# A windowed-attention and MLP kernel on one NeuronCore: the order replanned with later landings of batch 0's cast loads

## The chip, the cores and the metric

The kernel runs on one core of one Trainium2 chip. The metric is the device time of one execution in microseconds, lower being better; the figure for the kernel before is the median of 13 executions. The profile is of one further execution of the same program. Its engines are TensorE (PE; PEld is its weight load), VectorE (DVE), ScalarE (ACT), GpSimd (POOL) and SyncE (SP).

## The reference

Attention over 4 batches, 8 heads, 768 positions and head size 64, where each query sees the last 128 keys and the first 4 ("sinks"), is followed by a two-layer MLP with a squared ReLU on the 3072 tokens of 512 features:

```python
scores = scale * q @ k^T
keep   = (key position < 4) | (0 <= query - key < 128)
a      = softmax(where(keep, scores, -1e9))
x      = (a @ v), heads side by side: 3072 x 512
h      = x @ w_in                      # 512 -> 2048
out    = (max(h, 0) ** 2) @ w_out      # 2048 -> 512
```

All inputs and the output are float32.

## The kernel before

**Tiling.** A batch has six tiles of 128 positions, taken as three tile pairs (`s` or `u` = 0, 1, 2). For each batch the stages are: bring q and k into a layout with the head size on the partitions (`stage`, by PE transposes for batches 0 and 1 and by DMA transposes on SP's queue for 2 and 3); scores, exponential and mask; values and normalisation; the "bridge", which transposes the attention output for the MLP; `layer1` with ReLU and square; and `layer2`. Most of layer 2 is done by `layer2_fast`, which forms a tile pair with seven block products in place of eight, from sums of the squares (`sg`) and of the weights (`wt`). Attention of batch b+1 is interleaved with the MLP of batch b.

**Who does what.** PE runs all matmuls and transposes. ACT has the exponentials and most ReLUs; DVE has the normalisations, most squares, sums and copies out of PSUM. A multiplication by the window mask can be on DVE (L776) or on POOL (a pair of affine selects, L355). `sink_keys` (two small copies into `kblk`, L679) gathers the keys of the four sinks, `sink_scores` (L703) multiplies by them, `sink_exp` (L711) is their exponential, and every value product of tile pairs 1 and 2 reads the result. PSUM is divided into four tiles of two banks, two named "att" and two named "den".

**Loads.** q and k of batch 0, tiles 0 to 3, come as float32 through SP's queue and are cast ("regrouped") on DVE, ACT or POOL. Tiles 4 and 5 of batch 0 and all of the other batches, as v, w_in and w_out, are cast to bfloat16 by DMAs that POOL issues. `load_cast` issues those of q and k for batches 0 (tiles 4 and 5) and 1 (L507). The POOL queue's order is fixed by the program: v tiles 0 and 1, a quarter of w_in, v 2 and 3, the other three quarters of w_in, k and q tiles 4 and 5, v 4 and 5, w_out, and then batch 1. The DMAs of a queue follow one another in that order; where POOL's compute instructions stand between them is the planner's choice.

**What sets the order.** Nothing in the program is placed by hand at the end. Every piece of work is an `Op` with a key, the engines that can do it with an assumed cost, the ops that it follows and the buffers that it takes and frees. `Plan.run` repeatedly takes, of all ops that are ready, the one with the lowest (planned start + lag, key), chooses the engine that would end it first, and emits its instructions. `Plan.place` first moves the keys and lags: by group with `PLACES` (a shift, a scale and a lag for all ops of, say, the scores of batch 1's tile pair 0), and then one by one with `NUDGES`. The assumed times are only for planning: `LATENCY` is the assumed handoff between engines, and a DMA is assumed to land at

```python
end = queue[e] + DMA_LATENCY + o.margin
```

(L238). So the constants change no instruction by themselves; they change the order on each engine and the engine that some ops get. One thing depends on planned gaps directly: `warm` (L317) emits PE transposes of the identity, which compute nothing that is used, in front of an op for which PE is planned to wait, as long as the planned time is below `WARM_UNTIL`.

The function that the diff touches:

Of the kernel before, what the change touches and what calls it, by code (L numbers as in the profile page):

```python
# [16 lines left out]
LATENCY = 0.122  # L17
# [5 lines left out]
    ('att', 0, 0): (-2.46, 0.47, -0.66), ('att', 0, 1): (-0.14, 1.62, -0.14), ('att', 0, 2): (-1.375, 1.42, -0.64),  # L23
    ('att', 1, 0): (0.765, 0.89, 0), ('att', 1, 1): (-0.28, 2.29, -0.72), ('att', 1, 2): (0.08, 1.3, -0.06),
    ('att', 2, 0): (-0.07, 1.27, 0), ('att', 2, 1): (1.14, 0.56, -0.28), ('att', 2, 2): (-1.285, 1.05, -0.48),
    ('att', 3, 0): (0.09, 1.14, 0.06), ('att', 3, 1): (0.4, 1.06, -0.08), ('att', 3, 2): (-0.465, 1.16, -0.56),
    ('ev', 0, 2): (-0.46, 0.74, 0.02), ('ev', 1, 0): (-0.01, 0.91, -2.78), ('ev', 1, 1): (-0.165, 1.04, 0),
    ('ev', 1, 2): (-0.025, 0.87, 0.02), ('ev', 2, 0): (0.11, 0.96, 0), ('ev', 2, 1): (-0.045, 0.93, 0.36),
    ('ev', 2, 2): (-1.3, 0.62, 1.04), ('ev', 3, 0): (0.22, 2.01, -1.96), ('ev', 3, 1): (0, 1, -0.42),
    ('ev', 3, 2): (0.04, 1.07, -0.02), ('l1', 0, 0): (-0.28, 2.16, -0.32), ('l1', 0, 1): (-0.035, 0.33, -0.46),  # L30
    ('l1', 0, 2): (1.69, 0.27, -0.42), ('l1', 1, 0): (0.825, 0.61, -0.02), ('l1', 1, 2): (-0.155, 0.96, 0.14),
    ('l1', 2, 0): (0.035, 0.76, -0), ('l1', 2, 2): (-2.375, 1.53, -0.32), ('l1', 3, 0): (0.025, 1.07, -0.42),
    ('l2', 0, 0): (0.32, 2.21, -0.22), ('l2', 0, 1): (0.44, 1.69, 0.06), ('l2', 0, 2): (-4.315, 2.49, -0.54),
    ('l2', 1, 0): (0, 1.01, 0), ('l2', 1, 1): (2.345, 1.97, 0.22), ('l2', 1, 2): (-0.41, 0.56, 0.12),
    ('l2', 2, 0): (-0.41, 0.41, -0.6), ('l2', 2, 1): (-0.47, 0.26, 0.66), ('l2', 2, 2): (0, 1.01, 0),
    ('l2', 3, 0): (-0.09, 1.06, 0), ('l2', 3, 2): (-0.12, 0.72, 2.76), ('prep', 0, 0): (4.54, 2.5, -1),
    ('prep', 0, 1): (-1.04, 0.71, -0.64), ('prep', 1, 0): (0.935, 2.5, -0.44), ('prep', 3, 0): (-0.495, 2.45, 0.1),
    ('sink', 0, 0): (-0.755, 0.62, -0.54), ('sink', 0, 1): (0.135, 0.98, -0.04),
    ('sink', 1, 0): (-0.375, 1.71, 0.04), ('sink', 1, 1): (0.365, 0.61, 0.08), ('sink', 2, 0): (-0.01, 2.21, 0.06),
    ('sink', 3, 0): (-0.045, 0.9, 0), ('sum', 0, 2): (0, 1, -0.2), ('sum', 1, 0): (0.345, 0.25, -2.82),  # L40
    ('sum', 1, 1): (-0.27, 0.85, 0.08), ('sum', 1, 2): (-0.61, 0.73, -0.3), ('sum', 2, 0): (-0.06, 0.53, 1.32),
    ('sum', 2, 1): (-0.185, 1.13, 0.06), ('sum', 2, 2): (1.225, 2.25, -1.82), ('sum', 3, 0): (-0.005, 0.78, -0.5),
    ('sum', 3, 1): (-0.08, 0.34, 0.58), ('sum', 3, 2): (-0.185, 1.76, 0.42), ('turn', 0, 0): (4.705, 1.71, -0.76),
    ('turn', 0, 1): (0.09, 1.27, -0.04), ('turn', 0, 2): (1.185, 0.93, -0.3), ('turn', 1, 0): (0, 1.04, 0),
    ('turn', 1, 1): (0.995, 1.58, 0.4), ('turn', 1, 2): (0.65, 0.38, 0.02), ('turn', 2, 0): (0.67, 0.92, 0.14),
    ('turn', 2, 1): (-0.005, 0.93, -1.56), ('turn', 2, 2): (0.105, 1.4, 0.26), ('turn', 3, 0): (-0.1, 1.13, 0.08),
    ('turn', 3, 1): (-0.045, 0.55, -0.08), ('turn', 3, 2): (0.095, 1.46, -0.1),
    ('val', 0, 0): (-3.365, 0.71, -0.66), ('val', 0, 1): (0.145, 1.37, 0), ('val', 0, 2): (-1.82, 0.34, -3),
    ('val', 1, 0): (-0.355, 1.14, 0.04), ('val', 1, 1): (1.24, 2.09, -0.76), ('val', 1, 2): (0.18, 1.66, -2.5),
    ('val', 2, 0): (4.08, 1.76, -1.82), ('val', 2, 1): (0.05, 1.41, 0), ('val', 3, 0): (-1.585, 0.72, -0.38),  # L50
    ('val', 3, 1): (0.115, 0.58, -0.88), ('val', 3, 2): (-0.1, 1.09, -0.02), ('wt', 0): (0.275, 0.55, 0.32),
}
NUDGES = {
    4: (-0.366, 1.44), 16: (0, -0.3), 17: (0.072, -1.02), 18: (-0.061, -1.08), 19: (0.005, -0.02),
    20: (0.18, -0.98), 21: (0.025, -1.52), 24: (0, -0.44), 25: (-0.338, -1.38), 26: (0.71, 1.9),
    27: (-0.006, -0.32), 28: (0.484, 0.84), 29: (0, -0.36), 30: (-0.027, 0.14), 31: (0.007, -0.26), 32: (0, -0.48),
    33: (-0.136, -2.88), 34: (-0.096, 0.58), 35: (-0.031, 0.88), 36: (-0.018, 0), 37: (0.103, 0.12),
    39: (0.084, 0.7), 41: (-0.017, 0.88), 42: (0, -0.36), 43: (-0.11, 0.72), 44: (0, -0.12), 45: (0.297, 0.68),
    46: (-0.172, -1.86), 47: (-0.011, 0), 48: (-0.112, -0.02), 49: (-0.039, 1.08), 50: (-0.207, 0.22),
    51: (-0.044, 1.66), 52: (-0.002, -0.14), 53: (-0.017, -1.04), 54: (0, -0.2), 56: (-0.203, 0.34),  # L60
    58: (0.029, -0.48), 59: (0.008, 0), 60: (0.204, -1.22), 61: (0.19, 0.54), 62: (-0.101, -1.14), 63: (-0.022, 0),
    64: (0.192, 0.18), 65: (-0.153, 0.14), 66: (0.306, 0), 67: (0, -0.12), 69: (0.192, -2.78), 70: (-0.072, 0),
    71: (-0.012, 0), 72: (0, 0.38), 73: (-0.071, -0.04), 74: (-0.001, 0.16), 75: (-0.154, 0.08), 76: (0.133, -0.02),
    77: (0.57, 1.32), 78: (0.012, 0.46), 81: (-0.043, 0.3), 82: (0.016, -2.06), 83: (0.261, -0.22), 84: (-0.009, 0),
    86: (0.047, -0.02), 87: (0.257, -0.48), 88: (-0.361, 0.4), 89: (-0.047, 0.42), 90: (0.15, 0.34),
    91: (-0.217, 0), 92: (0, -0.06), 93: (0.05, -0), 94: (-0.016, 0), 95: (0.007, 0.02), 98: (0.071, -1.36),
    99: (-0.204, 0.84), 100: (0.062, -0.24), 101: (0, 0.08), 102: (0.126, 0.34), 103: (-0.194, -0.22),
    104: (0.051, 0), 105: (-0.214, -0.16), 108: (0.126, 0), 109: (0.206, 0), 110: (0.582, 0.28), 111: (0.032, 0.44),
    113: (-0.082, 0.1), 114: (-0.531, 0.32), 115: (0.058, -0.02), 116: (-0.003, -0.42), 118: (0.141, -1.44),
    119: (-0.307, 0.3), 120: (0.009, 0.06), 121: (0.002, 0), 122: (-0.044, 0.36), 123: (-0.017, 0.24),  # L70
    125: (-0.069, 0.34), 126: (0.099, -0.44), 127: (0, 0.14), 128: (-0.238, -0.62), 129: (-0.154, -0.08),
    130: (-0.003, 0), 131: (-0.296, 0.4), 132: (-0.082, -0.32), 133: (0.024, -0.38), 134: (0.073, 0),
    135: (0.059, 0.06), 136: (0.065, 0), 137: (0.021, 0.44), 138: (-0.166, 0.68), 139: (0.012, 0.3),
    140: (0.032, -0.28), 141: (-0.189, 0), 143: (0.103, 0), 144: (0.071, -0.44), 145: (-0.059, 0),
    146: (-0.436, 0.38), 148: (0.164, -0), 150: (0.527, -1.46), 151: (-0.19, 0.24), 153: (0.033, 0), 155: (0, 0.04),
    156: (0.089, 0), 157: (0.185, -0.32), 158: (-0.173, 0.56), 159: (-0.171, 0.18), 160: (0.252, 0.52),
    161: (-0.034, 1), 162: (-0.113, 1.42), 163: (0.013, 0.48), 165: (-0.127, 0.32), 166: (0.044, 0.4),
    167: (-0.035, 0.68), 169: (0, -0.14), 170: (-0.137, 0), 171: (-0.007, 0.26), 172: (0, 0.16),
    174: (-0.066, -0.92), 175: (0.19, 0.58), 177: (0.091, 0), 178: (0.319, -0.4), 179: (-0.18, 1.08),
    180: (-0.069, 0.02), 181: (-0.338, 0.2), 182: (-0.006, -0.02), 185: (-0.471, 1.5), 186: (-0.092, 0),  # L80
    187: (0.214, -0.08), 188: (0.107, -0.42), 189: (0.232, 0), 190: (0.088, 0), 192: (0, -0.16), 193: (-0.003, 0),
    194: (-0.01, -0.06), 196: (0.202, -0.16), 197: (0.001, -0.26), 198: (-0.511, 0), 199: (0.009, -1.34),
    200: (0.532, 0.1), 201: (-0.061, -1.16), 202: (-0.007, 0), 204: (-0.154, 0.18), 205: (0.379, 0.36),
    206: (-0.08, 0.86), 208: (0.012, -1.06), 209: (-0.163, -1.22), 210: (-0.013, 0), 211: (0.032, 0.04),
    212: (-0.121, 0), 213: (0, -0.2), 214: (0, 1.06), 215: (0, -0.06), 216: (0.121, 0.78), 217: (-0.108, 0),
    218: (0.25, 0.48), 219: (-0.155, 0), 220: (0.299, -0.24), 221: (0, -0.16), 222: (0, -0.3), 223: (-0.2, 0),
    224: (-0.065, 0), 225: (0, -0.38), 226: (0.019, -0.14), 228: (0.152, -0.9), 229: (-0.183, -0.86),
    230: (-0.164, 0), 231: (-0.021, 0.6), 232: (0.141, 0.18), 233: (-0.345, 0.26), 236: (0.132, -2.36),
    237: (0.017, -0.1), 238: (0, 0.72), 239: (-0.152, 0.14), 240: (-0.106, 0.48), 241: (-0.058, 0.3),
# [165 lines left out]
def kernel(  # L255
# [239 lines left out]
    def load_cast(b, tiles):  # L495

        for ti in (1, 0):
            for t in tiles:
                takes = []
# [726 lines left out]
```

## Time and profile before

| | us |
|---|---|
| median of 13 executions (216.68 to 217.8) | 217.06 |
| profiled execution, its own time | 217.19 |
| its span, from the first to the last instruction | 215.5 |
| PE busy in the span | 206.8 |
| DVE busy | 146.0 |
| ACT busy | 117.6 |
| POOL busy | 88.7 |

The profiled execution took 0.13 us more than the median, and 1.7 us of its time lie outside the span. Rows of the profile give the engine, the line of the kernel that made the instruction (which can be that of a helper: L331 is any copy on DVE, L329 any on ACT), what it writes and reads, and the times. A PE's end is modelled, so its busy time is an upper bound of the work. Waits name what ended them.

### The profile page before, as it was taken

To read this page: it belongs to the slowest core of one execution; us is meant where nothing else is said; L and a number is where in the kernel's file an instruction comes from. 1 tells how busy PE (TensorE), PEld (TensorE's weight loads), DVE (VectorE), ACT (ScalarE), POOL (GpSimd) and SP (SyncE) were. 2 spreads that over 40 slices of the span, in tenths; PEclk is the share of its full clock that TensorE was granted. 3 is DMA by queue.
4 is the path that set the end of the run, shared out by engine and by line. 5 is a ranking of instruction groups with operands and counts; after the bars stand their busy time and mean duration, and the time that the engine had idled before them with its cause. 6 is when DMAs were issued, how large, how long until landed. Compare 5 with 4: busy or idle time off the path is not lost.

```text
span 215.5 us, 5189 instructions
## 1 busy us (share of the span) xinstructions
PE 206.8 (96%) x2184; PEld 160.1 (74%) x2184; DVE 146.0 (68%) x276; ACT 117.6 (55%) x147; POOL 88.7 (41%) x127
## 2 busy tenths in 40 slices
PE   7789999999999999999999999999999999999992
PEld 7548987688667688554889765884988855799892
DVE  6588546697965866966788858779984543466652
ACT  3588667548864267778651627668411036656210
POOL 7999273598988963089405002227000000000000
PEclk9999999999999999999999999999999999999999
DMA  5999999999999999999969976020152220000222
GB/s 161 275 184 206 170 204 212 157 132 191 159 131 160 188 154 197 150 123 104 146 45 158 160 173 148 6 46 0 27 76 97 97 101 0 0 5 0 97 100 97
DMA packets 93351, 26.06 MB, mean 121 GB/s; under 512 B 86800, under 2 KB 91280, under 8 KB 93328
## 3 DMA queue, kind: packets, MB, share of 16 engines
q0 software_dynamic: 69248, 12.59, 76.4%
q1 hardware_dynamic: 23896, 13.07, 29.2%
q8 instruction: 17, 0.28, 0.5%
q10 hardware_dynamic: 184, 0.07, 0.1%
q14 instruction: 6, 0.05, 0.1%
HBM read 27.30 MB, written 6.29 MB: 156 GB/s over the span
## 4 chain that ended last, share of the span: by engine, by line
PE 81%; DMA 7%; POOL 4%; DVE 3%; SPq 1%; ACT 1%; issue 1%; POOLq 0%
PE pm L890 35%; PE py L1042 28%; PE py L931 6%; PE po L812 6%; DMA qn<-in_q_dram 5%; PE ps L744 4%; DMA qr<-in_k_dram 3%; SPq L486 1%; POOL qn L507 1%; PE pt L637 1%; POOL w_in_sb L443 1%; DVE qkT L331 1%; PE ya L1042 1%; PE px L861 1%; DVE r L903 1%
## 5 line engine op out<-in xcount | busy, mean ns | idle before, releaser
L890 PE MATMUL pm<-xT,w_in_sb 128*128 128x256 bf16 (+1 forms) x576 | 88.3, 309 | 0.3 <-ACT r L901 0.2
L890 PEld LDWEIGHTS <-w_in_sb 128*128 128x128 bf16 x576 | 62.4, 114 | 20.7 <-issue 2.1
L901 ACT ACTIVATE r<-pm 128x1024 bf16<-128x1024 f32 x41 | 42.0, 1024 | 39.4 <-PE pm L890 37.9
L764 ACT ACTIVATE expm<-ps 128x1024 bf16<-128x1024 f32 (+1 forms) x48 | 43.4, 951 | 12.0 <-PE ps L744 11.8
L912 DVE TENSOR_TENSOR gT<-r 128x1024 bf16<-128x1024 bf16 x34 | 24.1, 711 | 20.9 <-ACT r L901 20.5
L355 POOL TENSOR_SCALAR_AFFINE_SELECT expm<-expm 128x512 bf16<-128x512 bf16 x26 | 18.1, 722 | 44.7 <-ACT expm L764 37.3
L1042 PEld LDWEIGHTS <-gT 128*128 128x128 bf16 x336 | 31.3, 98 | 3.7 <-issue 0.3
L1042 PEld LDWEIGHTS <-sg 128*128 128x128 bf16 x240 | 22.8, 98 | 3.9 <-issue 0.9
L1042 PE MATMUL py<-wt,sg 128*128 128x256 bf16 x160 | 20.8, 273 | 0.1
L1042 PE MATMUL py<-wt,gT 128*128 128x256 bf16 x160 | 20.7, 273 | 0.0
L1042 PE MATMUL py<-w_out_sb,gT 128*128 128x256 bf16 x144 | 18.7, 273 | 0.0
L829 DVE TENSOR_TENSOR xn_sb<-po,rc 128x512 bf16<-128x512 f32 (+1 forms) x28 | 17.2, 615 | 1.0
L812 PEld LDWEIGHTS <-expm 128*128 128x128 bf16 x352 | 16.3, 97 | 1.8 <-issue 0.5
L812 PE MATMUL po<-v,expm 128*128 128x65 bf16 x352 | 17.2, 193 | 0.0
L776 DVE TENSOR_TENSOR expm<-expm,tri 128x1024 bf16<-128x1024 bf16 x19 | 13.2, 710 | 4.6 <-ACT expm L764 4.6
L931 PE MATMUL py<-w_out_sb,gT 128*128 128x512 bf16 x64 | 15.8, 380 | 0.0
L744 PE MATMUL ps<-qkT 64*128 64x128 bf16 (+1 forms) x256 | 14.8, 238 | 0.2 <-DVE xn_sb L829 0.2
L910 ACT ACTIVATE gT<-r 128x1024 bf16<-128x1024 bf16 x14 | 14.7, 1058 | 0.3
L744 PEld LDWEIGHTS <-qkT 64*128 64x128 bf16 x256 | 8.0, 94 | 7.8 <-issue 5.4
L329 ACT ACTIVATE osb<-py 128x256 f32<-128x256 f32 (+1 forms) x13 | 5.6, 433 | 13.2 <-PE py L1042 7.7
L812 PE MATMUL po<-vs,es 128*128 128x65 bf16 x128 | 12.6, 193 | 0.0
L545 POOL DMA_DIRECT2D v<-in_v_dram x12 | 10.7, 908 | 4.0 <-PE po L812 4.0
(79 smaller groups left out, 243.5 us busy)
## 6 DMA issues: line engine op xcount, KB each, us to landing
out_dram<-osb SPq DMA_DIRECT2D x11, 512.0 KB, 3.8
v<-in_v_dram POOLq DMA_DIRECT2D x24, 128.0 KB, 6.1
qn<-in_k_dram POOLq DMA_DIRECT2D x20, 128.0 KB, 7.2
qn<-in_q_dram POOLq DMA_DIRECT2D x20, 128.0 KB, 6.3
w_in_sb<-in_moe_w_in_dram POOLq DMA_DIRECT2D x4, 512.0 KB, 8.7
w_out_sb<-in_moe_w_out_dram POOLq DMA_DIRECT2D x4, 512.0 KB, 10.7
qr<-in_k_dram SPq DMA_DIRECT2D x4, 256.0 KB, 5.5
qr<-in_q_dram SPq DMA_DIRECT2D x4, 256.0 KB, 5.3
```

What stands on the lines that cost most here:

```text
L355: nc.gpsimd.affine_select(out=e_tile, in_=e_tile, compare_op=ALU.is_ge, fill=fill, base=i - 1, pattern=[[0, n], [1 if i else -1, 128]], ch ...
L744: nc.tensor.matmul(ps[:, h2, o:o + w], lhsT=qkT_sb[r, m, 1, c, :], rhs=qkT_sb[r, m, 0, qb:qb + w // 128, :], start=(i == 0 and not biased) ...
L764: nc.scalar.activation(out=x[:, :, o:512], in_=bank_t["s", b, s, m][:, :, o:512], func=AF.Exp, scale=scale)
L776: nc.vector.tensor_mul(y, y, tri.rearrange("p (o a) c -> p o (a c)", o=1).to_broadcast([128, 4, 256]))
L812: touch(("po", b, s, m0), e, nc.tensor.matmul(pv[:, i, h2, :], lhsT=lhsT, rhs=rhs, start=(n_ == 0), stop=(n_ == len(mms) - 1)), j)
L829: touch(("po", b, s, m0), e, nc.vector.tensor_tensor(out=xn_sb[:, 2 * s:2 * s + 2, 128 * (m0 + j0):128 * (m0 + j0 + nj)].rearrange("p i (j ...
L890: nc.tensor.matmul(pm[:, i, :], lhsT=w_in_sb[:, fb // 4, kb, fb % 4:512:4], rhs=xT[:, c0 // 256:(c0 + cw) // 256, kb, :], start=(kb == 0), ...
L901: nc.scalar.activation(out=o, in_=h, func=AF.Relu)
L910: nc.scalar.activation(out=g, in_=r, func=AF.Square)
L912: nc.vector.tensor_mul(g, r, r)
L931: touch((b, u), e, nc.tensor.matmul(pm[:, i, :], lhsT=gT_sb[t // 4][:, fb, 128 * (t % 4):128 * (t % 4) + 128], rhs=w_out_sb[:, fb, :], sta ...
L1042: ins = nc.tensor.matmul(y_, lhsT=x[:, i, :], rhs=r_, start=(first or tail and n == 2) and i == 0, stop=i == HB - 1, skip_group_check=not ...
```

## The change

The diff has three parts. `LATENCY`, the assumed handoff, goes from 0.122 to 0.135 us. The loads of `load_cast` get a margin: they are assumed to land 1.2 us later for batch 0 and 0.3 us later for batch 1. And `PLACES` and `NUDGES` are new throughout: another set of shifts and lags, so that the order on every engine is another one.

```diff
-LATENCY = 0.122
+LATENCY = 0.135
...
 PLACES = {
-    ('att', 0, 0): (-2.46, 0.47, -0.66), ('att', 0, 1): (-0.14, 1.62, -0.14), ('att', 0, 2): (-1.375, 1.42, -0.64),
...
+    ('att', 0, 0): (3.3, 1.08, 0.18), ('att', 0, 1): (3.285, 0.47, 0.38), ('att', 0, 2): (-0.2, 1.41, -0.24),
...
 NUDGES = {
-    4: (-0.366, 1.44), 16: (0, -0.3), 17: (0.072, -1.02), 18: (-0.061, -1.08), 19: (0.005, -0.02),
...
+    4: (-0.022, 0.56), 16: (0, 0.14), 17: (-0.211, -0.38), 18: (0.48, -1.62), 19: (0, 0.4), 20: (0.364, -0.58),
...
-                dma_op("pool", ("qk", b, ti, t), run, 0.9, None, takes)
+                dma_op("pool", ("qk", b, ti, t), run, 0.9, None, takes).margin = 0.3 if b else 1.2
```

What this does to the order, read from the two programs' instructions:

- The set of PE operations is the same; there are 61 warm-up transposes in place of 56. DVE has 239 planned operations in place of 233, ACT 148 in place of 146, POOL 86 in place of 94.
- Start: k and q of head pair 1 are transposed ahead of those of pair 2. POOL no longer casts k of head pair 3 (DVE does). On POOL, the triangles and the first window mask stand ahead of w_in 2 and 3 (the quarters are numbered from 0); they stood behind w_in 2. `sink_scores` of batch 0 moves from ahead of three of the four scores of tile pair 1 to behind all four, and `sink_exp` to behind three exponentials on ACT. The transposes of tiles 4 and 5 move behind one more layer-1 group.
- Batch 0, layer 2: tile pair 1 comes first, then pair 0 with pair 2; before, it was pair 0, then pair 1 with pair 2. SP's first store is now that of tile pair 1, and the store of tile pair 0 stands third, ahead of eight DMA transposes for batch 2.
- Batch 1: attention goes through tile pairs 0, 1 and 2 in that order; before, it was 1, 2, 0. Six of its eight first-group transposes stand together.
- Batches 2 and 3: the layer-2 pairs and the attention pieces are interleaved in another order. The last seven products, their evacuations and the last store are the same.

## The prediction

> **What bounds the kernel now.** I read the page's busy rows and slices first, then TensorE's waits, then the busy time by stretch, then the timelines of the first 30 us.
>
> ```profile
> span 215.5 us, 5189 instructions
> PE 206.8 (96%) x2184; PEld 160.1 (74%) x2184; DVE 146.0 (68%) x276; ACT 117.6 (55%) x147; POOL 88.7 (41%) x127
> PE   7789999999999999999999999999999999999992
> PEclk9999999999999999999999999999999999999999
> ```
>
> TensorE is busy for 96% of the span, at the full granted clock, and the slices below 9 are the first three and the last. All four batches' matmuls stay, so a new order can only take away time in which TensorE stands still, or add some. How much there is:
>
> ```profile
> PE pt L322 <- POOL ident L379: 1.5, 1, 1.5
> PE pt L637 <- DVE qs L331: 1.4, 1, 1.4
> PE pk L703 <- DVE kblk L679: 0.6, 1, 0.6
> PE pt L637 <- DMA qn<-in_q_dram: 0.5, 1, 0.5
> PE px L861 <- DVE xn_sb L829: 0.3, 1, 0.3
> PE pm L890 <- ACT r L901: 0.2, 1, 0.2
> PE ps L744 <- DVE xn_sb L829: 0.2, 1, 0.2
> ```
>
> Columns: who waited for whom, us in total, times, longest. All but the 0.2 for `r` lie before 30 us, and the stretches agree:
>
> ```profile
> 4.25:17.45 13.20, 10.74 (x148) 7.00 (x146) 9.29 (x20) 9.34 (x14) 12.43 (x22) 1.00 1.46 229
> 17.45:30.00 12.55, 12.09 (x156) 11.87 (x153) 6.94 (x20) 8.37 (x11) 7.75 (x11) 1.00 1.72 188
> 30.00:50.00 20.00, 20.00 (x215) 14.83 (x213) 14.42 (x24) 11.98 (x14) 13.68 (x19) 1.00 1.76 171
> 50.00:90.00 40.00, 39.65 (x471) 30.22 (x471) 29.95 (x57) 25.90 (x33) 28.54 (x37) 1.00 2.08 168
> ```
>
> Each row is a stretch, its length, then busy us of PE, PEld, DVE, ACT, POOL. PE idles 2.46 us from 4.25 to the first MLP matmul at 17.45, 0.46 from there to 30, 0.35 in 50 to 90, and nothing in the later stretches up to 211.5. So at most about 3.3 us can be won, most of it before 17.5 us, while the later 180 us can only lose. Three places matter before 30 us:
>
> ```profile
> 12.48 2.06 DVE L679 COPY kblk<-qkT 64x16 bf16<-64x16 bf16 x2
> ...
> 12.76 0.58 POOL L355 TENSOR_SCALAR_AFFINE_SELECT tri<-tri 128x128 bf16<-128x128 bf16 x2
> 13.27 1.23 POOL L355 TENSOR_SCALAR_AFFINE_SELECT expm<-expm 128x512 bf16<-128x512 bf16 x2
> ...
> 11.18 3.10 ACT L764 ACTIVATE expm<-ps 128x1024 bf16<-128x1024 f32 x4
> ...
> 28.97 0.45 PE L637 MATMUL pt<-ident,qn 128*128 128x128 bf16 x5 [0.46 <-DMA qn<-in_q_dram]
> ```
>
> (Start, us, instruction, [idle before it].) The two tiny sink-key copies take 2.06 us, until 14.54, while the same pair of batch 1 takes 0.83 (timeline, 55.97). The four normalisations behind them, each 0.6 (RECIPROCAL 0.17, TENSOR_TENSOR 0.42), start only at 14.57; they end at 16.84, and the bridge, its copies and layer 1 follow. The last line is the cast load of q tile 5, landing 28.93, for which TensorE stood 0.46.
>
> **The change, part by part.** The margin and LATENCY add no instruction: they alter planned times, and with the new PLACES and NUDGES the order. In instructions: the PE work is the same but for 61 warm-up transposes in place of 56, all before layer-1 group 4 of batch 0; about twice as many go where a wait was planned, so I price them at nothing in a wait and 5 x 0.06 = 0.3 at most. POOL loses its one CAST (0.6) and, net, seven mask pairs (1.23 each, 0.69 on DVE); DVE gains 6 operations and ACT 2. Neither DVE (68%) nor ACT (55%) becomes the bound by that.
>
> *To the first layer-1 matmul.* The transposes now come in the order in which q and k land (m0, m1, m2, m3, where m2's k stood ahead of m1). That fills the 1.4 us wait, but the last q load, regrouped on ACT at 10.64 (0.63), still gates m3's transposes (11.3 against 11.43), and v tile 1 lands at 12.46, where the first value product starts in both. So the 1.4 is worth nothing by itself: the landing and the exponentials are late next. ACT's four exponentials follow the regroup as before (11.2 to 14.4; with one done early and the bridge copy at 14.75). What moves is POOL and DVE. POOL no longer regroups; the triangles follow w_in 1 and run at about 11.0 to 11.5, and the mask on expm waits for its exponential, now third in ACT's row: 12.9 to 14.2. DVE reaches the sink keys at 12.4; the second copy starts at about 12.85, takes 0.17 to 0.43, and the norms go at 13.1, 13.7, 14.4 (behind its value product) and 15.1 (behind the exponential ending 14.5). From there: second bridge half 15.75 to 16.0, scores to 16.35, sink scores to 16.7, xT copy 16.55, layer 1 at 16.7 against 17.45. The sink exponential moved behind three others on ACT: 18.05 to 18.45, and all four value products of tile pair 1 need it, so they start at 18.5 where layer 1 left off at 18.45. Four of them at 0.365, with two warm-ups: second layer-1 group at 20.05 against 20.69, which is **-0.64**.
>
> One rule speaks against this. The row: 2.06 us for a pair that elsewhere takes 0.83, ending with POOL's last select at 14.50. The Trainium skill, "SBUF — State Buffer", section "Who interferes with whom", says a VectorE copy in a two-port mode and a GpSimd operation take a shared port pair as a lock, and the one issued later waits for the whole of the other. The row agrees (1.2 us longer), though a mask product at 62.52 under a POOL select took 0.88 against 0.68, less than a full wait. By the row alone the lock is gone with the overlap: -0.64. By the rule it depends on who starts first, copy at 12.85 or select at 12.9; if the select wins, norms start at 14.25, layer 1 at 17.7, the sink exponential at 19.25, the values at 19.7 and the next group at 21.2: +0.5. I take the first, since the copy is ahead by a hair.
>
> *To 30 us.* One more 1.75 us layer-1 group stands ahead of the tile-4/5 transposes, which come at about 29.3 (20.05 and 0.45 of bridge, then five groups at 1.75), behind the landing at 28.93. The 0.46 goes: **-0.46**. If the lock holds, the work is later by itself and 0.5 - 0.46 leaves 0.
>
> POOL's queue, which this reordering passes: w_in 2 and 3 were issued at 12.01 and 15.38 and now stand behind that mask, at about 14.2 and 15. The queue was behind (w_in 1 landed 19.08, w_in 2 21.69), and the shortest issue to landing seen on it is 4.1 (56.59 to 60.65), of which 0.85 is its own service: an issue before 19.08 - 3.2 = 15.9 delays nothing. Cost 0. The deadlines are 22.3 and 25.8.
>
> *30 to 211.5.* Here the order of batch 0's layer 2, and of batch 1 to 3, is new. The small waits of before (0.07 at 57.6, 0.20 at 78.4, 0.08 at 85.6) belong to their old neighbours: -0.35. New ones, by the order: six transposes now stand together before batch 1's sink scores; DVE has a relu (1.2), three copies (0.4), two squares (0.6 to the next start) and the key copies (0.83), 4.5 us, and waits 0.9 for the transposes between, 5.4 in all, against 5.27 of PE work (1.75 + 6 x 0.225 + 2 x 0.865 + 0.44) from the end of that relu's matmuls: +0.15. Bridge of batch 1's tile pair 0 to its layer 1, with only scores and sinks between: +0.15. Batch 2's second value product takes an "att" buffer that the bridge of batch 1 frees one copy (0.42) later, with 0.37 of work between its end and the handoffs: +0.33. These three are not in the trace of before; I bound them by 0 and 1.5 together, and take 0.63, near the waits of its own kind (0.07 to 0.6). Sum **+0.28**.
>
> SP: the store of batch 0's tiles 0 and 1 moves from first to third, behind matmuls at about 71, and eight DMA transposes queue behind it; at 1.3 to 2.2 issue each and 6.3 to land the fourth is there at about 86, needed at 94. Free. Layer 2's w_out tiles are wanted 3 us after they land (32.48, 34.94, 37.39, 39.84). The last product, its evacuations and stores have one order in both: the 3.9 us tail stays.
>
> Sum: -0.64 - 0.46 + 0.28 = -0.82. Against the profiled execution's 217.19 (span 215.5) that is 216.37; the runs' median lies 0.13 lower, 217.06, so **216.25**.
>
> **The rivals.**
> A. The lock holds: sink keys still end with the mask. For it: 0.05 us between the two starts. Against: POOL is idle from the triangles. Time: 217.06 + 0.0 + 0.28, about 217.3.
> B. Slower, by one mechanism: the w_in loads. If w_in 2's later issue is passed on whole (14.2 - 12.0 = 2.2 us), it lands at 23.9 and not at 22.3 where it is wanted, everything behind it in the queue shifts too, and q tile 5 lands at 31.1 against 29.3: +1.8 for -1.1 won, 217.06 + 0.7 + 0.28, about 218.0. It decides from an issue later than 15.9. Against it: the backlog.
> C. The batch-1 block, 46 to 95 us, gives the gain back: the three new waits reach their bound of 1.5, and VectorE's queue slips once by a relu (1.2) in front of a copy that TensorE needs: 217.06 - 1.1 - 0.35 + 2.7, about 218.3. For it: PE has only four tiles of PSUM to run ahead in. Against: before has busier stretches of DVE (29.95 of 40 us there) with 0.35 of idle.
> That the change doesn't do what it says: the load lands no later; only the plan thinks so. The 0.46 shows that it was right to.
>
> **How the numbers follow.** Forecast 0.5 (own range 215.5 to 216.8), A 0.2, B 0.15, C 0.15. About 0.2%, 0.43 us, is what a measurement can tell here from no change. Faster by more: most of the forecast, 0.44, and 0.02 of A, 0.46. Within: 0.05, 0.13, 0.01, 0.02, about 0.21. Slower: 0.33, from A's upper part, B and C. Range 215.5 to 218.1: it leaves out what lies beyond B and a gain past 1.5.
>
> **What would show it.** Right: key copies of about 0.8 in all ending before 13.3, layer 1 at about 16.7, no wait on qn near 29, the PE rows after 30 us idle by 0.3 to 0.9. Wrong: key copies of 2 us (A); a wait of PE on w_in at 22 or 26 (B); PE idle over 1.5 us between 46 and 95 (C).

## The result, and the profile after

The changed kernel takes 215.83 us (median of 11 runs, 215.01 to 216.39; one further run on record, outside the median, took 216.84) against 217.01 for the kernel before (48 runs). The ratio is 0.9941, with a 95% interval of 0.9928 to 0.9954: faster by 0.6%. The profiled execution took 215.88 us. Every profile below is likewise of one of the runs of its kernel.

The page's first rows: the span, the busy time of each engine, and TensorE's busy tenths by slice.

```profile
span 214.1 us, 5183 instructions
PE 206.3 (96%) x2189; PEld 159.9 (75%) x2189; DVE 146.6 (68%) x282; ACT 119.0 (56%) x149; POOL 78.5 (37%) x112
PE   7699999999999999999999999999999999999992
```

The span is 1.4 us shorter: TensorE stands still 0.9 us less (7.8 in place of 8.7) and is busy 0.5 us less; as the ends of matmuls are modelled, the split is rough. Its waits (who waited for whom, us in total, times, longest) and the busy time by stretch (length, then busy us of PE, PEld, DVE, ACT, POOL) say where:

```profile
PE pt L327 <- POOL ident L384: 1.5, 1, 1.5
PE pt L642 <- DVE qs L336: 1.5, 1, 1.5
PE pt L327 <- ACT expm L769: 0.3, 1, 0.3
PE pm L895 <- DVE xT L336: 0.2, 1, 0.2
PE po L817 <- DVE xT L336: 0.2, 1, 0.2
```

```profile
4.25:16.70 12.45, 10.42 (x151) 6.80 (x149) 7.60 (x21) 9.22 (x14) 10.61 (x17) 1.00 1.43 222
16.70:30.00 13.30, 13.30 (x171) 13.22 (x168) 9.07 (x23) 8.04 (x10) 10.04 (x15) 1.00 1.70 188
30.00:50.00 20.00, 20.00 (x211) 14.84 (x209) 15.60 (x22) 11.43 (x15) 13.98 (x20) 1.00 1.80 178
50.00:90.00 40.00, 39.81 (x434) 26.28 (x432) 28.90 (x56) 27.61 (x37) 27.48 (x35) 1.00 2.11 170
90.00:150.00 60.00, 59.85 (x628) 46.72 (x627) 43.31 (x79) 40.56 (x49) 12.24 (x17) 1.00 0.94 96
```

The rows for `kblk`, `xn_sb`, `qn` and `r` are gone from the waits; 16.7 to 50 us has no idle time at all. The last three rows are new: the 0.3 lies at 10.9 us, the last two behind 70 us. Three timelines (start, us, instruction, [idle before it]) show the two places that the prediction named, VectorE and GpSimd at the sink keys and TensorE at the transposes of tiles 4 and 5:

```profile
12.78 0.34 DVE L684 COPY kblk<-qkT 64x16 bf16<-64x16 bf16 x2
13.24 0.18 DVE L833 RECIPROCAL rc<-po 128x4 f32<-128x4 f32 x1
```

```profile
11.21 0.54 POOL L360 TENSOR_SCALAR_AFFINE_SELECT tri<-tri 128x128 bf16<-128x128 bf16 x2
13.36 1.22 POOL L360 TENSOR_SCALAR_AFFINE_SELECT expm<-expm 128x512 bf16<-128x512 bf16 x2 [1.61 <-ACT expm L769]
14.53 0.76 POOL L448 DMA_DIRECT2D w_in_sb<-in_moe_w_in_dram  x1
```

```profile
29.33 1.06 PE L642 MATMUL pt<-ident,qn 128*128 128x128 bf16 x16
30.22 1.91 PE L895 MATMUL pm<-xT,w_in_sb 128*128 128x256 bf16 x16
32.06 0.61 PE L749 MATMUL ps<-qkT 64*128 64x128 bf16 x12
```

The key copies take 0.34 us in place of 2.06 and the norms follow at 13.24. All sixteen transposes stand together behind the landing (28.82) and wait for nothing.

How far after is ahead is read from the start times of the same matmuls in the two traces: 0.67 us at the first layer-1 matmul (16.78 against 17.45), 0.60 at the fifth layer-1 group (25.83 against 26.43), 1.40 at the last product (209.925 against 211.327).

### The profile page after: what moved, and what is told of

Read it like the earlier page. It is cut to its first block, busy times and chain, and to the rows that moved or that the text cites. A ratio compares the mean times of both kernels' runs of the same rounds, so it can differ in the third digit from the quotient of the medians.

```text
span 214.1 us, 5183 instructions
## 1 busy us (share of the span) xinstructions
PE 206.3 (96%) x2189; PEld 159.9 (75%) x2189; DVE 146.6 (68%) x282; ACT 119.0 (56%) x149; POOL 78.5 (37%) x112
## 4 chain that ended last, share of the span: by engine, by line
PE 92%; DMA 3%; SPq 2%; DVE 1%; ACT 0%; issue 0%; ACTq 0%
PE pm L895 40%; PE py L1047 28%; PE po L817 7%; PE py L936 7%; PE ps L749 5%; DMA qr<-in_q_dram 3%; PE pt L642 2%; SPq L491 2%; PE px L866 1%; PE ya L1047 1%; PE pk L708 1%; DVE xT L336 1%; PE ps L742 0%; ACT qs L334 0%; PE po L327 0%
## 5 line engine op out<-in xcount | busy, mean ns | idle before, releaser
L895 PE MATMUL pm<-xT,w_in_sb 128*128 128x256 bf16 (+1 forms) x576 | 87.4, 308 | 0.2 <-DVE xT L336 0.2
L906 ACT ACTIVATE r<-pm 128x1024 bf16<-128x1024 f32 x42 | 43.0, 1024 | 31.7 <-PE pm L895 29.6
L360 POOL TENSOR_SCALAR_AFFINE_SELECT expm<-expm 128x512 bf16<-128x512 bf16 x12 | 7.3, 632 | 74.7 <-ACT expm L769 69.7
L781 DVE TENSOR_TENSOR expm<-expm,tri 128x1024 bf16<-128x1024 bf16 x26 | 18.2, 705 | 7.7 <-ACT expm L769 7.6
L334 ACT ACTIVATE osb<-py 128x256 f32<-128x256 f32 (+1 forms) x15 | 6.6, 441 | 16.8 <-PE py L1047 11.7
L915 ACT ACTIVATE gT<-r 128x1024 bf16<-128x1024 bf16 x13 | 13.7, 1056 | 0.3
L817 PEld LDWEIGHTS <-es 128*128 128x128 bf16 x128 | 11.7, 97 | 0.0
```

The source lines that it names most:

```text
L360: nc.gpsimd.affine_select(out=e_tile, in_=e_tile, compare_op=ALU.is_ge, fill=fill, base=i - 1, pattern=[[0, n], [1 if i else -1, 128]], ch ...
L781: nc.vector.tensor_mul(y, y, tri.rearrange("p (o a) c -> p o (a c)", o=1).to_broadcast([128, 4, 256]))
L817: touch(("po", b, s, m0), e, nc.tensor.matmul(pv[:, i, h2, :], lhsT=lhsT, rhs=rhs, start=(n_ == 0), stop=(n_ == len(mms) - 1)), j)
L895: nc.tensor.matmul(pm[:, i, :], lhsT=w_in_sb[:, fb // 4, kb, fb % 4:512:4], rhs=xT[:, c0 // 256:(c0 + cw) // 256, kb, :], start=(kb == 0), ...
L906: nc.scalar.activation(out=o, in_=h, func=AF.Relu)
L915: nc.scalar.activation(out=g, in_=r, func=AF.Square)
```

## The experiments

The question was whether the parts of the change can be had one at a time. Each kernel replays a written-down order in place of the planner's choice; with the list of before or after it emits that kernel's instructions in the same order on every engine. Each ratio is against runs of before made alongside. Work is named by the planner's numbers. About 30 us these are: 131 and 128 the PE transposes of tiles 4 and 5 (eight matmuls each), 136, 145 and 144 scores of tile pair 2, and 177, 171 and 165 layer-1 groups of 1.75 us. TensorE's order there:

```
before: 128 177 136 131 171 144 145 165
after:  177 131 128 165 136 145 171 134 289 144
```

In the texts of expectations, "pin" is the theory that the landings of cast loads fix the end whatever is won ahead of them; its opposite is that the terms of the sum add.

**b_seam**: before, one layer-1 group moved ahead of the transposes.

```diff
-128 177 136 131 171 144 145 165
+177 128 136 131 171 144 145 165
```

> The order of before, with one layer-1 group (feature blocks 12 to 15 of tile pair 1) moved ahead of the transposes of tiles 4 and 5 and nothing else. Theory (pin): in before everything behind 28.93 us hangs on the landing of q tile 5; with 1.75 us of other work in front, the transposes start at about 29.9 and do not wait, and the 0.46 wait with its pipeline refill (0.63 from start to start) goes: 0.3% faster, 216.4. Rival (sum: the start and the landing are independent gains): the same 0.63. Rival (the landing matters nothing, the middle's new order made the gain): no change, and a wait somewhere later takes the 0.63 back.

Measured: 217.31 us, ratio 1.0006 (0.9985 to 1.0026), not the 216.4 expected. The timeline of TensorE shows why nothing was won:

```profile
30.12 0.61 PE L661 MATMUL pt<-ident,qn 128*128 128x128 bf16 x8
30.56 0.55 PE L346 MATMUL ps<-ident 128*128 128x128 bf16 x7
31.19 0.40 PE L768 MATMUL ps<-qkT 64*128 64x128 bf16 x6
```

The wait for the load is gone. But scores 136 now follow the transposes at once, and the transposes' result has first to be copied out of PSUM: seven warm-up transposes and a wait stand there, 31.19 - 30.56 = 0.63 us, as much as the landing wait had cost (0.62 from start to start, see below).

**b_keys**: before, with the triangles ahead of the w_in loads on GpSimd.

```diff
-w_in 1, w_in 2, triangles, mask
+triangles, w_in 1, w_in 2, mask
```

> The order of before, with the two triangle selects on POOL moved ahead of w_in 1 and 2 so that no POOL select runs while DVE copies the sink keys. The two copies should take 0.4 to 0.9 in place of 2.06 and the first layer-1 matmul start 0.6 to 1.1 us earlier, at 16.4 to 16.9. Theory (pin): the total does not move (within 0.1%), because the wait on q tile 5 near 28 us grows from 0.46 by the same amount. Rival (sum): 0.6 to 1.1 us faster. If the copies still take 2 us, the lock was not what made them long.

Measured: 217.09 us, 1.0005 (0.9989 to 1.002). The key copies take 0.75, end at 13.73, and layer 1 starts at 16.65, 0.80 earlier than in before. TensorE then waits for three landings:

```profile
20.32 1.94 PE L914 MATMUL pm<-xT,w_in_sb 128*128 128x256 bf16 x16 [0.27 <-DMA w_in_sb<-in_moe_w_in_dram]
22.93 5.43 PE L914 MATMUL pm<-xT,w_in_sb 128*128 128x256 bf16 x48 [0.17 <-DMA w_in_sb<-in_moe_w_in_dram]
29.15 0.45 PE L661 MATMUL pt<-ident,qn 128*128 128x128 bf16 x5 [0.63 <-DMA qn<-in_q_dram]
```

At the last it is 0.18 us behind before, where the matmul after the wait starts at 28.97. The first two waits had already used up the start's gain: of the 0.80, 0.36 is left at the second layer-1 group and 0.01 at the third (22.93 against 22.94). The wait for q tile 5 then costs what it cost in before, and a little more.

**b_keys_seam**: both edits.

> Both moves together in the order of before. Pin: 0.63 from the landing plus what the start gives, 1.2 to 1.6 us faster (215.4 to 215.8), with no or a short wait on q tile 5: the two together are worth more than the sum of the two alone. Sum: each alone already showed its part, and together the sum of the two.

Measured: 217.16 us, 0.9994 (0.9974 to 1.0015), not the 215.4 to 215.8 expected. It has the loss behind the transposes of b_seam and a w_in wait of 0.15. Its key copies took 1.56 us, though the triangles were long done: a first sign against my reading of that row.

**a_seam_back**: after, with the transposes moved back ahead of a layer-1 group.

```diff
-177 131 128 165
+131 128 177 165
```

> The order of after, with the transposes of tiles 4 and 5 put back ahead of that layer-1 group. Pin: they come up at 27.6, wait for the landing at 28.9, and the whole gain is lost but for the middle: 1.2 to 1.4 us slower than after, about 217.0. Sum: only the 0.46 to 0.63 of the landing is lost, 216.4.

Measured: 217.1 us, 0.9999 (0.9983 to 1.0015). This one edit takes the whole 0.6% away, with after's start and after's order of everything behind. In its profile the start is 0.31 us ahead of before at the fifth layer-1 group, since TensorE had waited 0.6 us for `w_in` loads by then. TensorE's timeline shows eight warm-up transposes and the wait for the load:

```profile
27.87 0.61 PE L351 MATMUL pt<-ident 128*128 128x128 bf16 x8
28.32 0.33 PE L666 MATMUL pt<-ident,qn 128*128 128x128 bf16 x3
28.84 0.90 PE L666 MATMUL pt<-ident,qn 128*128 128x128 bf16 x13 [0.19 <-DMA qn<-in_q_dram]
```

**b_seam2**: before, with a group ahead of the transposes and one behind them.

```diff
-128 177 136 131 171 144 145 165
+177 131 128 171 136 144 145 165
```

> The order of before with the whole passage around the cast transposes as after has it: one layer-1 group first, then both transposes (tile 4/5 of all four head pairs), then another layer-1 group, and only then the scores that read the transposes' copies; the ReLUs and squares of the groups ahead of the copies. 56 warm-ups as in before. In the first try, with only the one group moved, the landing's 0.63 was gone and 0.62 came back as a wait for ACT's copy with seven planned warm-ups in front of the scores. Theory (cover): with a group between transposes and scores the 0.63 stays won: 216.4. Rival (the passage is neutral, the gain came from the later order): 217.0.

Measured: 217.44 us, 1.0022 (1.0002 to 1.0042), not the 216.4 expected. Now three scores stand in a row, and the third waits for an exponential to free a PSUM tile named "att":

```profile
30.68 1.91 PE L914 MATMUL pm<-xT,w_in_sb 128*128 128x256 bf16 x16
32.52 0.62 PE L768 MATMUL ps<-qkT 64*128 64x128 bf16 x12
34.03 0.40 PE L768 MATMUL ps<-qkT 64*128 64x128 bf16 x6 [0.90 <-ACT expm L788]
```

**a_start_b_rest**: the order of after up to the last work before 177, then before's.

> The order of after up to the last common layer-1 group at 26 us, then the order of before for all that is left. Theory (pin): the better start is lost at the landing of q tile 5 (28.8 to 29.1) and the total is that of before within 0.1%, 217.0. Sum: 0.55 faster, 216.5.

Measured: 217.17 us, 1.0009 (0.9988 to 1.0029). In the runs the start alone is worth nothing. How it is lost this profile cannot show, for it is of the slowest of the twelve runs (218.35): v tile 1 landed at 13.48 and not, as in after, at 12.88, TensorE waited 1.26 for it, and layer 1 started at 17.39, hardly before the 17.45 of before. Waits of 0.24 and 0.23 for w_in and of 0.32 for the q load followed.

**a_start_seam2_b_rest**: the same start with b_seam2's passage.

> The start of after, the passage at 26 to 34 us as in the run above (group, both transposes, group, scores), then the order of before for all the rest, some 175 us. If the gain of after lies ahead of 34 us, this has all of it: 1.1 to 1.3 faster than before, 215.7 to 215.9. If the later order of after is worth something, it is missing here; the passage alone plus the start would then stop at 216.4.

Measured: 217.01 us, 1.0007 (0.9983 to 1.0031), not the 215.7 to 215.9 expected. There is no wait for the q load, and again 0.90 in front of the third score (at 33.80). A lead from the start (0.37 at the fifth layer-1 group) and the transposes without a wait are both had here up to 31 us; most of it is given back at one badly placed score, and 0.14 is left at the last product.

**b_seam3**: before, with a passage in which a group stands between each producer and its consumer.

```diff
-128 177 136 131 171 144 145 165
+177 131 128 171 136 145 165 144
```

> The kernel before in its own order, with one passage about 30 us rearranged: the layer-1 group 177 stands ahead of both transposes of tiles 4 and 5 (131, 128), group 171 between the transposes and the scores, two scores (136, 145) together, group 165, and only then the third score (144). Nothing else moves, the start of before stays. Theory 'passage': the gain behind 29 us is had when a group of 1.75 us stands between each producer and its consumer, the landing wait (0.63 start to start) goes and is not given back: 217.0 - 0.6 = 216.4, ratio 0.997; no wait over 0.1 us on TensorE between 28 and 36 us. Rival 'pin': the end of before is set by the landings of the cast loads, whatever the order about 30 us, so 217.0, ratio 1.000, with a new wait further on. Rival 'shape': the rearranged scores cost refills of their own, 217.3.

Measured: 216.99 us, 0.9995 (0.9971 to 1.002): no gain is resolved, and the interval reaches down to the 0.997 expected. Its profile has no wait over 0.1 us between 28 and 36, and TensorE is 0.63 us ahead of before's trace at 36 us. Then 0.22 goes at the sink scores, which stand right behind the exponential that they need, and 0.26 at a cast load of batch 1 (wait 0.09 at 48.6); at the last product 0.12 is left. The 0.63 is the passage's own, because at the fifth layer-1 group this profile is level with before, though its layer 1 started at 16.14, 1.30 earlier. TensorE stood for the landing of w_in 1:

```profile
20.39 1.94 PE L914 MATMUL pm<-xT,w_in_sb 128*128 128x256 bf16 x16 [0.71 <-DMA w_in_sb<-in_moe_w_in_dram]
```

The 1.30 came without an edit: with before's order up to there, the key copies took 0.89 us in this run.

**a_start_seam3_b_rest**: that passage with after's start.

> The start of after (up to the last piece of work before group 177), the rearranged passage of b_seam3, and the rest of the order of before. Theory 'passage': both gains are had, 0.55 to 0.64 ahead of the second layer-1 group and 0.63 at the landing, less what waits for w_in loads take (0.1 to 0.3): 215.8 to 216.1, ratio 0.995; that would be as fast as after although nothing behind about 36 us is changed. Rival 'pin': 216.4, the same as b_seam3, because what is won at the start is waited for again. Rival 'middle': after wins by its order of batches 1 to 3, and this stays at 216.8 or above.

Measured: 216.33 us, 0.9964 (0.9944 to 0.9984). TensorE's timeline:

```profile
29.03 1.06 PE L661 MATMUL pt<-ident,qn 128*128 128x128 bf16 x16
29.92 1.91 PE L914 MATMUL pm<-xT,w_in_sb 128*128 128x256 bf16 x16
31.77 0.62 PE L768 MATMUL ps<-qkT 64*128 64x128 bf16 x12
32.31 1.94 PE L914 MATMUL pm<-xT,w_in_sb 128*128 128x256 bf16 x16
34.18 0.39 PE L768 MATMUL ps<-qkT 64*128 64x128 bf16 x6
```

It is 1.53 us ahead of before at 36 us, 1.31 behind the sink scores and 1.32 at the last product. This profile is of the fastest of the twelve runs (216.00), so its 1.32 is more than the kernel gains as a rule; by the ratios 0.36% of after's 0.59% is there with before's order of batches 1 to 3. The theory had said 215.8 to 216.1, the "pin" 216.4. The runs lie nearer the second, but not for its reason: their median is 0.66 us below that of b_seam3, so the start is not waited off.

**b_start_a_rest**: before's start, after's order from the transposes on.

> The start of before, with its sink keys behind the masks, and from the transposes of tiles 4 and 5 on the order of after. Theory 'passage': the landing wait is won and the start's gain is missing: 217.0 - 0.63 = 216.4, ratio 0.997, with layer 1 starting at about 17.4. Rival 'pin': what counts is being behind the landing at 29 us and not the start, so this is as fast as after, 215.8, ratio 0.994. Rival 'start': the start is all of the gain, so this is 217.0.

Measured: 216.76 us, 0.9974 (0.9952 to 0.9997). In the profiles it is 0.61 us behind after at the transposes and 0.62 at the last product: a lead ahead of the passage goes through undiminished once the passage has no wait. The lead is not one of order alone. Layer 1 started here at 16.22, not at the 17.4 expected and earlier than in after; the key copies took 0.89 us, not 2.06, with GpSimd's instructions in before's order:

```profile
12.41 0.89 DVE L708 COPY kblk<-qkT 64x16 bf16<-64x16 bf16 x2
```

```profile
12.70 0.58 POOL L384 TENSOR_SCALAR_AFFINE_SELECT tri<-tri 128x128 bf16<-128x128 bf16 x2
13.20 1.24 POOL L384 TENSOR_SCALAR_AFFINE_SELECT expm<-expm 128x512 bf16<-128x512 bf16 x2
```

Then w_in 1 and 2 landed at 20.29 and 22.88, about 0.97 later than in after, and the layer-1 groups that read them started at 20.33 and 22.93. With a_start_b_rest and b_seam3 this gives a table of ratios:

| | before's passage | rearranged passage |
|---|---|---|
| before's start | 1 | 0.9995 (b_seam3), 0.9974 (with after's rest) |
| after's start | 1.0009 (a_start_b_rest) | 0.9964 (a_start_seam3_b_rest), 0.9941 (after) |

With the rearranged passage, after's start is worth 0.31% (with before's rest) and 0.33% (with after's), of which the second is clear of the noise. After's order of the rest is worth 0.21% and 0.23%, neither clear of it.

**a_lock**: after, with the w_in loads ahead of the selects, so that the triangles meet the key copies.

```diff
-w_in 1, triangles, mask, w_in 2, w_in 3
+w_in 1, w_in 2, w_in 3, triangles, mask
```

> The order of after with w_in 2 and 3 issued ahead of the triangles and the first mask on POOL (they came behind), so that POOL's selects run while DVE copies the sink keys. Theory (lock): the two copies take 1.4 to 2.0 in place of 0.34, the first layer-1 matmul moves from 16.8 to about 17.7, the next group from 20.1 to about 21.1, and the wait that hid in the landing does not absorb it all: 0.4 to 0.9 slower than after, 216.2 to 216.7. Rival (w_in): the earlier issue of w_in 2 and 3 brings their landing forward and the time stays or falls. Rival (slack): the 0.4 us between the transposes and the landing of q tile 5 takes half of it.

Measured: 216.18 us, 0.9966 (0.9945 to 0.9988). VectorE's and GpSimd's timelines:

```profile
12.70 0.34 DVE L708 COPY kblk<-qkT 64x16 bf16<-64x16 bf16 x2
```

```profile
10.38 2.27 POOL L472 DMA_DIRECT2D w_in_sb<-in_moe_w_in_dram  x3
12.71 0.54 POOL L384 TENSOR_SCALAR_AFFINE_SELECT tri<-tri 128x128 bf16<-128x128 bf16 x2
```

The selects run beside both copies and lengthen neither. An overlap with selects is thus not enough for the 2.06 us of before. What every kernel with long copies had, and this one has not, is an issue of a w_in load running when the copies begin. The time is at the edge of the range expected for longer copies, but not by them: layer 1 started at 16.73, and then TensorE waited for w_in 2, which landed at 22.64:

```profile
22.69 7.18 PE L919 MATMUL pm<-xT,w_in_sb 128*128 128x256 bf16 x64 [0.22 <-DMA w_in_sb<-in_moe_w_in_dram]
```

**a_issue**: after, with w_in 2 and 3 issued behind the triangles, in GpSimd's gap.

```diff
-w_in 1, triangles, mask, w_in 2, w_in 3
+w_in 1, triangles, w_in 2, w_in 3, mask
```

> The kernel after with one thing moved: GpSimd issues the loads w_in 2 and w_in 3 directly behind the two triangle selects, so that an issue (0.76 each) is under way when VectorE copies the sink keys at about 12.8; in after GpSimd stands idle there. Before and its descendants, in which the second key copy took 0.58 to 1.63, all had a w_in issue running as the copies began; after and its descendants, with 0.17, had none, and a select beside the copies alone did not lengthen them (a_lock). Theory 'issue': the copies are held from an issue on through the select that follows: the pair takes 0.9 or more, layer 1 starts at 17.0 to 17.5 in place of 16.78, and the time is 216.1 to 216.5. Rival 'GpSimd's cast': what went with the long copies is that GpSimd also did a regrouping cast, absent here: the pair stays at 0.34, layer 1 at 16.8, 215.8 to 216.2. Either way the prediction's rival B is tested from the other side: issues 2 us earlier land w_in 2 at 21.9 or later all the same if the queue is behind, and by 19.7 if it is not.

Measured: 216.3 us (6 runs) against 217.55 for the before of that session, 0.9948 (0.9928 to 0.9968): not distinguishable from after. The same two timelines:

```profile
12.59 0.68 DVE L708 COPY kblk<-qkT 64x16 bf16<-64x16 bf16 x2
```

```profile
11.77 1.51 POOL L472 DMA_DIRECT2D w_in_sb<-in_moe_w_in_dram  x2
13.27 1.25 POOL L384 TENSOR_SCALAR_AFFINE_SELECT expm<-expm 128x512 bf16<-128x512 bf16 x2
```

The pair takes 0.68 us, between the two expectations. The first copy (0.15) is untouched; the second, from 12.76, takes 0.51 in place of 0.17 and ends at 13.27, where the second issue ends (13.28). So an issue on GpSimd can hold such a copy; the select that followed did not prolong it here. That it must hold one is not shown: the first copy ran wholly under an issue. Layer 1 starts at 16.83, because the value products that the norms wait for come no earlier. w_in 2, issued 2.8 us earlier than in after, landed at 22.64 and not at 21.91: the early issue bought nothing.

## Why the prediction was right

The forecast was 216.25 us and the result is 215.83: the sign and the two places of the gain were right, and the gain was larger than the sum: 1.18 us between the medians and 1.40 at the last product of the profiles, for 0.82. Of the three terms, one agrees in part by luck, one was too small and one had the wrong sign.

- **Start, predicted -0.64, measured -0.60** (at the fifth layer-1 group, in after's profile). Each step came within 0.2 us of its place: norms at 13.24, 13.80, 14.58 and 15.28, bridge half at 15.79, layer 1 at 16.78, the sink exponential at 18.12, the values at 18.64, the next group at 20.14. The wait for `qs`, which was to be filled without any gain, stayed (1.5).
- **The luck in it.** The loads were asked only whether they would land later, not how much of an earlier start they let through. In all 14 profiles w_in 2 landed 2.53 to 2.61 us behind w_in 1, whenever it was issued. In after it landed at 21.91 and the third layer-1 group started at 22.34 without a wait. In the six other profiles with after's start the group started 0.04 to 0.05 us behind that landing, at 22.01 to 23.97; at the fifth group four lie 0.03 to 0.37 us ahead of before, one 0.90 ahead and one 1.06 behind (a_start_b_rest). So 0.60 is the start's gain in one run with early landings; over the runs the start is worth the 0.3% of the table.
- **The rule weighed there.** Rival A rested on the lock that the Trainium skill, "SBUF — State Buffer", section "Who interferes with whom", states for a VectorE copy in a two-port mode and GpSimd: the one issued later waits for the whole of the other. Without overlap in after, the row decided: 0.34 us. Beside selects the copies took the same 0.34 (a_lock), so a full wait was not seen there; whether these copies run in such a mode no run shows. The experiments correct the cause that I took from the row: selects beside the copies are not enough for a hold (a_lock), and an issued load can start one (a_issue). What ends it is open. With one order of GpSimd's instructions, the second copy ended with the mask in before, b_seam and b_seam2 (14.54, 14.72, 14.39; it took 1.62, 1.63 and 1.16) and with the triangles in b_seam3 and b_start_a_rest (13.08 and 13.31; 0.58 each). So the 2.06 us are not a fixed cost of before's order.
- **Transposes, predicted -0.46, measured -0.63.** The term was mis-sized. I priced the wait by its idle time, 0.46. In before's trace the matmul behind it starts 0.68 after the one ahead of it, where two such matmuls otherwise start 0.06 apart: the wait cost 0.62. b_seam3 gains 0.63 by the passage alone, read at 36 us.
- **The loads, predicted 0: right for what was asked.** w_in 2 was issued 2.5 us later than in before and landed at 21.91 against 21.69, w_in 3 at 25.11 against 25.42; TensorE waited for neither in after's profile. The shortest time from issue to landing on that queue in before is 3.3 us (98.71 to 102.03), not 4.1; that moves the bound from 15.9 to 16.6 and changes nothing.
- **30 us to the end, predicted +0.28, measured -0.17** (1.40 less 0.60 and 0.63), so the sign was wrong. Two of the three new waits came where I had placed them: the bridge at 73.8 (idle 0.19) and the "att" buffer at 92.1 (0.15), together 0.34 idle for 0.48; at the key copies, the first, TensorE does not stand idle. What wins the rest back shows in no listed wait, and it was not found. The 0.21% and 0.23% of the table point the same way, unresolved as they are.
- **The rivals.** A: the copies took 0.34. B: no wait on w_in in after; where other kernels had one it came from no later issue (a_lock issued w_in 2 3.4 us earlier than after and waited 0.22). C: TensorE idles 0.34 us between 46 and 95, not over 1.5. That the load lands as before: 28.82 against 28.93, so the margin moved only the plan.

What the prediction did not see is that its terms are no independent terms. Alone, the start gives nothing (b_keys, a_start_b_rest), since TensorE meets the w_in loads from 20 us on and the q load at about 29; alone, moving the group gives nothing (b_seam), since what follows was not ready either. a_seam_back shows it from the other side: undoing one of the two takes both. "The 0.46 goes" was true only because the planner also put a layer-1 group between the transposes and the scores, and another piece ahead of the third score.

Open: what makes the loads land early or late. w_in 1 landed between 19.1 and 21.3 us in these profiles, in both starts, and one profile of a kernel cannot tell how much of a lead ahead of 24 us is its order and how much is this.

## What to carry to other kernels

When an engine that is 96% busy waits for a transfer, work moved ahead of the wait is worth something only if the work behind it is ready too: follow the new order for two or three pieces past the wait, through the copy out of PSUM and the buffer that the third piece needs, before counting the wait as won. Gains ahead of a landing were worth nothing here until the landing was covered, and then counted; so measure such parts together, in a two-by-two table. For an earlier start, ask of every load that it now comes nearer to not only whether it lands later, but when it lands in other runs. And price a wait from start to start, not by its idle time.

## What the runs showed of the hardware that was not expected

- A copy of 64x16 elements on VectorE took 0.15 to 0.17 us alone and with selects beside it and no issue. While GpSimd issued a load the two of a pair took 0.15 and 0.51 (a_issue). Where selects followed that issue the second took 0.58 to 1.63 us; with one and the same order of GpSimd's instructions 0.58 in two runs and 1.16 to 1.63 in three.
- The loads on GpSimd's queue came no earlier when issued earlier: w_in 2 was issued at 14.53, 11.77 and 11.12 us in after, a_issue and a_lock, and landed at 21.91, 22.64 and 22.64, each time 2.53 to 2.60 us behind w_in 1.
- A wait of 0.46 us cost TensorE 0.62 from start to start. Around one of 0.90 (b_seam2) two matmuls start 1.11 apart, where such neighbours are otherwise up to 0.11 apart: about 1.0.
